# A second output pair whose loads start as places come free, its sums in another place, and output operands at one distance

## The chip, the cores and the metric

The kernel runs on one core of a Trainium2 chip. The metric is the device time of one execution in microseconds. Three runs of the kernel before took 709.29, 709.85 and 711.43 us; the median is 709.85.

## The reference

Linear attention over 4 batches, 8 heads and 576 positions with head dimension 64 (`kv = k^T v`, `out = q kv`, normalised by its root mean square), then two feed-forward layers on the 2304 tokens of width 512. The first has a softmax-weighted hidden layer of 1024 with a layer norm; the second, which the change touches, is this:

```python
a = x @ w_a            # 2304 x 512 times 512 x 1536
b = x @ w_b
return (a * b @ w_out).astype(np.float32)   # 2304 x 1536 times 1536 x 512
```

All of it is float32. Every product is made of three matmuls on numbers split into a high and a low part (`h` times `h`, `h` times `l`, `l` times `h`).

## The kernel before, in words

Three stages follow one another on one core. The first works through 18 token tiles (attention, first layer); its transposed results go to DRAM in `x2d`. The second (`quad`, L719 on) makes `a * b` for three blocks of 768 tokens, `s` = 0, 1, 2, and six slices `j` of the hidden width. The third (`out_pair`, L889 on) multiplies by `w_out`.

In the second and third stage a 2 by 2 block product is made of seven products in place of eight, with sums of the operands' quarters: `XB11, XT1, XT2, XB21, XB22, XT3, XT4` on one side (`XB` are quarters, `XT` sums made of them: XT1 = XT3's quarter - XB11, XT2 = XB22 - XT1, XT4 = XB21 - XT2, and the last, `XT3`, the difference of two quarters), `WA11, WS1, WS2, WA12, WS4, WS3, WA22` on the other.

`quad(j, s, m)` is one of these block products: seven products of 6 matmuls with 384 columns (L715), of which the last, WA22 times XT4, is put off into the next `quad` (`close_quad`, after its third product). `m` = 0 gives `a`, `m` = 1 gives `b`; `times` then multiplies them (VectorE for the first quarter, GpSimd for the others, L756) and stores them in DRAM, `gd[s]` (L758, SP's queue). The tiles of `a` and `b` lie in two pools at the right end of SBUF.

`out_pair(k)` is the same for two token tiles: seven products of 18 matmuls with 256 columns (L886), nine pairs, `pairs` = (s, m) for s in 1, 2, 0. The operands of pair `k` are `g2[k, n]`, a high and a low tile each. Their quarters are loaded from `gd` into the low tile (`g_load`, L831), sums are made on VectorE (`g_steps`, the tiles `e`), the high part is a cast on ScalarE and the low part a subtraction on VectorE (`g_split`, L838 and L557). The pairs use two sets of places in turn: pair 0 has `ga` and places of the weights of stage two, pair 1 the places of `x0`, which is free after `quad(5, 0, 1)`, the last of stage two. `e` of pair 1 lies where `a` and `b` lay.

The order of the work is written out by hand. Each `quad` has six ticks and each `out_pair` six; `then(t4=[...])` hangs steps on a tick of the next `quad`, `ticks` does so for an `out_pair`. Each engine takes its instructions in that order, DMA issues (SP's, ScalarE's) included. The weights `w_out` come as seven sums from DRAM: three into `w1`, which lies in the pool `wo` where the tiles of `x1` lay, and four into `w2`, which lies in the place of `x2`; `half` splits one half of such a weight. The high part of WA22 has a place of its own (`last_hi`, `wo3`).

Of the kernel before, what the change touches and what calls it, by code (L numbers as in the profile page):

```python
# [8 lines left out]
F32 = mybir.dt.float32  # L9
F32R = mybir.dt.float32r  # L10
# [7 lines left out]
DRAM = bass.MemoryType.DRAM  # L18

P = 128  # L20

# [76 lines left out]
def tile_attention_moe(ctx, tc, q, k, v, g_norm, w_in, w_out, g_ln, w_a, w_b, w_out2, out):  # L100
    nc = tc.nc
# [4 lines left out]
    NP = H // 2  # L106
    NK = DM // P
    NF1 = DF1 // P
    NF2 = DF2 // P
    NTILE = NT // P  # L110
    NS = S // P
    FULL = NS * P
    REST = S - FULL
# [5 lines left out]
    TB = SB * P  # L119
    TH = TB // 2  # L120
    NSB = NTILE // SB
    NJ = NF2 // 2
# [18 lines left out]
    gd = [dram.tile([P, 4, SB // 2, NJ, P], F32, name=f"gd{s}") for s in range(NSB)]  # L141
# [4 lines left out]
    def pool(name, bufs, stack=left, side="left", **kw):  # L146
        if side == "right":
            kw["side"] = "right"
        if stack is psum:
            kw["space"] = PSUM  # L150
        return stack.enter_context(tc.tile_pool(name=name, bufs=bufs, **kw))

    def pool_r(name, bufs, stack=None):
        return pool(name, bufs, right if stack is None else stack, "right")
# [7 lines left out]

    wt = pool("wt", 1, top)
    tx = pool("tx", 2, top)
    pool_r("rpad", 1).tile([P, 248], F32, name="rpad")

    xl0 = pool_r("xl0", 1)

# [59 lines left out]
    wo = {}  # L228
# [321 lines left out]
    WA11, WA12, WS3, WA22, WS1, WS2, WS4 = range(7)  # L550
    XB11, XT1, XT2, XB21, XB22, XT3, XT4 = range(7)
    p2 = {}
# [3 lines left out]
    def subtract(eng, out, a, b):  # L556
        eng.tensor_tensor(out=out, in0=a, in1=b, op=ALU.subtract)  # L557
# [164 lines left out]
    def close_quad():  # L722
        if open_quad:
            open_quad.pop()()
# [75 lines left out]
    HD = DM // 2  # L800
    wo2 = {}
    g2 = {}
# [24 lines left out]
        wo2[n] = [t if t is None else t.rearrange("p (j d) -> p j d", j=NJ) for t in (hi, lo)]  # L827
        eng.dma_start(out=wo2[n][1].bitcast(F32), in_=w2d[:, n])

    def g_load(k, n, c=slice(0, NJ), t=None):  # L830

        s, m = pairs[k]
        t = g2[k, n][1].bitcast(F32) if t is None else t
        nc.sync.dma_start(out=t[:, c], in_=gd[s][:, (XB11, XT3, XB21, XB22).index(n), m, c])

    def g_split(k, n, src, c=slice(0, NJ)):
        return [
            lambda: nc.scalar.copy(g2[k, n][0][:, c], src()[:, c]),  # L838
            lambda: subtract(nc.vector, g2[k, n][1][:, c], src()[:, c], g2[k, n][0][:, c].bitcast(F32)),
        ]  # L840
# [4 lines left out]
    def g_steps(k):  # L845

        e = []

        def begin_():
            e.extend(p2["e"].tile([P, NJ, P], F32, tag=f"e{n}", name=f"e{n}") for n in range(2))  # L850
            d(0, XT3, XB11)()

        def d(out, a, b):
            at_ = lambda x: e[-1 - x] if x < 0 else g2[k, x][1].bitcast(F32)
            return lambda: subtract(nc.vector, e[out], at_(a), at_(b))

        def sp(n, at_=None):
            return g_split(k, n, g_raw(k, n) if at_ is None else lambda: e[at_])

        return [  # L860
            begin_, *sp(XB11), d(1, XB22, -1), *sp(XT1, 0), d(0, XB21, -2), *sp(XT2, 1), d(1, XB22, XT3),
            *sp(XB21), *sp(XB22), *sp(XT3, 1), *sp(XT4, 0),
        ]
# [160 lines left out]
    def all_of(steps):  # L1024
        for f in steps:
            f()
# [26 lines left out]
    side = [f for n in ORDER for f in x_split(0, n, lambda n=n: xf[n])]  # L1053
# [35 lines left out]
    left.close()  # L1089
    p2["x2"] = pool("x2", 1, rest)  # L1090

    t = p2["x2"].tile([P, 14 * TB + 32], F32R, tag="x", name="x2")
    t = t[:, :14 * TB].rearrange("p (h n c t) -> p h n c t", h=2, n=7, c=2)
    xs2[2] = [[t[:, h, n] for n in range(7)] for h in range(2)]

# [2 lines left out]
    now, later = by_need[:6], by_need[6:]  # L1098
    for n, (count, which) in enumerate(((1, now), (6, later), (5, now), (2, later))):
        where = pool(f"x1_{n}", 1)  # L1100
        for _ in range(count):
            part, n = which.pop(0)
            x1[part, n] = where.tile([P, 2, TH], F32R, tag=f"x{part}{n}", name=f"x{part}1_{n}")
    xs2[1] = [[x1[part, n] for n in range(7)] for part in "hl"]
    side = [f for n in ORDER for f in x_split(1, n, lambda n=n: xf[n])]
# [6 lines left out]
    side = x_steps(2)  # L1112
# [8 lines left out]
    for j in range(1, NJ - 1):  # L1121
        n = 2 * j + 2
# [16 lines left out]
    te = xl0.tile([P, 3, NJ, P], F32, tag="x3", name="te")  # L1139
    w1, w2 = [], []  # L1140

    def parts(to, t, count):
        size = NJ * HD
        to.extend(t[:, 16 + n * size:16 + (n + 1) * size] for n in range(count))

    def first_place():
        left.close()
        p2["wo"] = pool("wo", 1)
        parts(w1, p2["wo"].tile([P, 16 + 6 * NJ * HD], F32R, tag="w", name="wo1"), 6)
        g2[0, XT2] = place(p2["wo"], "g")  # L1150

    def second_place():
        parts(w2, p2["x2"].tile([P, 14 * TB + 32], F32R, tag="x", name="wo2"), 7)

    def place(where, tag):
        t = where.tile([P, 2, NJ, P], F32R, tag=tag, name="gw")
        return t[:, 0], t[:, 1]

    def g_next(k, n):
# [10 lines left out]
    def half(n, part, eng=nc.vector):  # L1170
        return hi_lo(wo2, n, eng, part)
# [18 lines left out]
    for n, k in ((XB11, 0), (XT1, 1)):  # L1190
# [5 lines left out]
        t1=[gl_(XB11, most), gl_(XT3, most)], t4=[gl_(XB22, most), gl_(XB21, most)], t6=early[:3],  # L1196
# [5 lines left out]
        t1=early[10:12], t3=[first_place], t4=[wl(WA11, w1, 0, nc.scalar), gl_(XB11, last), gl_(XT3, last), gl_(XB22, last), wl(WS1, w1, 1)], t5=[gl_(XB21, last)],  # L1202
# [3 lines left out]
        t2=half(WA11, 0), t3=[wl(WS2, w1, 2), *late_[:4]], t4=half(WA11, 1), t5=late_[4:8], t6=late_[8:],  # L1206
# [3 lines left out]
        t1=half(WS1, 0), t2=half(WS1, 1), t3=[second_place], t4=[wl(WA12, w2, 0, nc.scalar), *half(WS2, 0)],  # L1210
        t5=[wl(WS4, w2, 1, nc.scalar), *half(WS2, 1)], t6=[wl(WS3, w2, 2, nc.scalar), *g_split(0, XT2, lambda: te[:, 1])],
# [3 lines left out]
    def last_operands():  # L1215
        g2[0, XT3], g2[0, XT4] = (place(p2["w", part, 1], "w") for part in "hl")

    def next_loads():
        for n in range(7):
            g2[1, n] = [x0.tile([P, NJ, P], F32R, tag=f"x{part}{n}", name=f"g{part}") for part in "hl"]  # L1220
        for n in (XB11, XT3, XB22, XB21):
            g_load(1, n)

    then(
        t3=[*half(WA12, 0, nc.gpsimd), *half(WA12, 1, nc.gpsimd)],
        t4=[last_operands, *g_split(0, XT3, lambda: te[:, 2])],
        t6=[next_loads, *half(WS4, 0)],
    )
    quad(j, 0, 1)

    def last_places():
        close_quad()
        all_of([*half(WS4, 1), *half(WS3, 0)])
        wo_load(WA22, None, w2[6])
        ab.close()
        p2["o"] = pool_r("o", 5)
        p2["e"] = pool_r("e", 1)
# [10 lines left out]
    side = []  # L1248
    for k in range(len(pairs)):
        counts = [2, 2, 3, 4, 4, 3]  # L1250
        if k == 0:
            side += [*half(WS3, 1), *g_split(0, XT4, lambda: te[:, 0])]
            counts = [0, 4, 4, 4, 4, 2]
        if k + 1 < len(pairs):
            side += g_steps(k + 1)
        ticks = [[side.pop(0) for _ in range(min(n, len(side)))] for n in counts]
        if k == 0:
            ticks[3] += [last_hi, *half(WA22, 0, nc.gpsimd), *half(WA22, 1, nc.gpsimd)]
            out_pair(k, ticks, first_o, last_places)
        else:  # L1260
            out_pair(k, ticks)
# [34 lines left out]
```

## Time and profile before

| what | us |
|---|---|
| median of 3 runs | 709.85 |
| the profiled execution | 709.85 |
| its span, first to last instruction | 708.0 |
| TensorE busy | 677.0 (96%) |
| VectorE busy | 521.8 (74%) |
| GpSimd busy | 305.9 (43%) |
| ScalarE busy | 294.3 (42%) |
| TensorE output products (L886) on the chain that ended last | 17% |

Stage two begins at 285.57 us of the span, the first output product at 566.93, and the last matmul ends at 704.74. The share of busy time counts a matmul from its start to its modelled end, so matmuls overlap in it; how fast they follow each other is read from a window's length and the number of matmuls in it. A wait shows as idle time in front of an instruction, with what released it.

### The profile page before, as it was taken

What the parts mean: (1) busy time and instruction counts of PE and PEld (TensorE: products, weight loads), DVE (VectorE), ACT (ScalarE), POOL (GpSimd) and SP (SyncE); (2) the same over time, 40 slices, a digit from 0 to 9 for tenths busy, and PEclk for the clock granted to TensorE, in tenths of its full rate; (3) what the DMA queues carried; (4) which work ended last, traced back from release to release, by engine and by line L of the source; (5) the groups of instructions that cost most, each with busy time, mean ns of one, the idle gap of its engine ahead of it and who ended that gap; (6) DMA issues with size and microseconds to landing.
All of it is one profiled execution on the core that took longest, in us unless ns stands there. A gap on an engine that the chain in (4) does not pass through costs nothing.

```text
span 708.0 us, 12282 instructions
## 1 busy us (share of the span) xinstructions
PE 677.0 (96%) x4550; PEld 647.8 (91%) x4550; DVE 521.8 (74%) x928; ACT 294.3 (42%) x507; POOL 305.9 (43%) x448
## 2 busy tenths in 40 slices
PE   2599999999999999999999999999999998999998
PEld 2488899999999898899999999999999998999998
DVE  3889977676688776778666866677647979878882
ACT  3668955544455346542321122211222535433431
POOL 2578775677666311114554465554652412000000
PEclk9889999999999999999999999999999999999999
DMA  9997745545542412352434346444345674544521
GB/s 247 315 249 210 191 130 166 153 120 162 165 128 75 135 45 68 105 155 67 143 106 145 116 119 195 141 144 148 116 136 156 241 267 120 158 119 136 148 73 56
DMA packets 107131, 103.83 MB, mean 147 GB/s; under 512 B 25280, under 2 KB 94400, under 8 KB 107072
## 3 DMA queue, kind: packets, MB, share of 16 engines
q1 hardware_dynamic: 101312, 95.18, 45.9%
q10 hardware_dynamic: 5760, 7.87, 3.3%
q8 instruction: 36, 0.59, 0.3%
q14 instruction: 23, 0.19, 0.1%
HBM read 71.05 MB, written 31.98 MB: 146 GB/s over the span
## 4 chain that ended last, share of the span: by engine, by line
PE 76%; DVE 10%; issue 4%; POOL 4%; ACT 3%; DMA 2%; SPq 0%; ACTq 0%; DVEq 0%; POOLq 0%
PE pw L715 28%; PE pq L886 17%; PE x2p L532 5%; PE x2p L530 5%; PE x2p L531 5%; PE ph L445 4%; PE ph L443 4%; PE ph L444 4%; PE ltp L500 2%; PE po L381 1%; PE kvp L349 1%; POOL a L756 1%; DVE nu L92 1%; DMA ring<-in_moe_w_in_dram 1%; PE xtp L418 1%
## 5 line engine op out<-in xcount | busy, mean ns | idle before, releaser
L756 POOL TENSOR_TENSOR a<-b,a 128x384 f32<-128x384 f32 x53 | 63.1, 1205 | 125.0 <-DVE b L745 124.1
L715 PE MATMUL pw<-xh,wh 128*128 128x384 f32 x336 | 114.3, 340 | 1.1 <-DVE b L766 0.3
L715 PE MATMUL pw<-xh,wl 128*128 128x384 f32 x336 | 112.9, 336 | 0.0
L715 PE MATMUL pw<-xl,wh 128*128 128x384 f32 x336 | 112.9, 336 | 0.0
L715 PE MATMUL pw<-x,wh 128*128 128x384 f32 x336 | 85.6, 335 | 0.1
L530 PE MATMUL x2p<-lh,woh 128*128 128x256 f32 x288 | 82.4, 286 | 0.3 <-ACT lh L510 0.2
L531 PE MATMUL x2p<-ll,woh 128*128 128x256 f32 x288 | 80.4, 279 | 0.8 <-DVE ll L513 0.8
L532 PE MATMUL x2p<-lh,wol 128*128 128x256 f32 x288 | 80.4, 279 | 0.5 <-DVE wol L49 0.5
L715 PEld LDWEIGHTS pw<-xh,wh 128*128 128x128 f32 x336 | 63.1, 188 | 4.9 <-DVE b L745 1.6
L715 PEld LDWEIGHTS pw<-xl,wh 128*128 128x128 f32 x336 | 63.1, 188 | 0.0
L715 PEld LDWEIGHTS pw<-xh,wl 128*128 128x128 f32 x336 | 63.1, 188 | 0.0
L715 PEld LDWEIGHTS pw<-x,wh 128*128 128x128 f32 x336 | 60.6, 188 | 0.7 <-DVE b L745 0.4
L886 PE MATMUL pq<-wo,gh 128*128 128x256 f32 x336 | 59.9, 280 | 0.0
L445 PE MATMUL ph<-wih,xl 128*128 128x512 f32 x144 | 57.5, 399 | 1.8 <-DVE xl L428 1.8
L443 PE MATMUL ph<-wih,xh 128*128 128x512 f32 x144 | 58.2, 404 | 0.1
L444 PE MATMUL ph<-wil,xh 128*128 128x512 f32 x144 | 57.4, 399 | 0.0
L715 PE MATMUL pw<-x,wl 128*128 128x384 f32 x168 | 56.2, 334 | 0.0
L531 PEld LDWEIGHTS x2p<-ll,woh 128*128 128x128 f32 x288 | 54.2, 188 | 1.2 <-DVE ll L513 1.2
L530 PEld LDWEIGHTS x2p<-lh,woh 128*128 128x128 f32 x288 | 54.4, 189 | 0.9 <-ACT lh L510 0.5
L886 PE MATMUL pq<-wo,gw 128*128 128x256 f32 x450 | 55.1, 280 | 0.0
L532 PEld LDWEIGHTS x2p<-lh,wol 128*128 128x128 f32 x288 | 54.3, 188 | 0.9 <-DVE wol L49 0.9
L886 PEld LDWEIGHTS pq<-wo,gw 128*128 128x128 f32 x450 | 54.0, 188 | 0.0
(155 smaller groups left out, 1563.8 us busy)
## 6 DMA issues: line engine op xcount, KB each, us to landing
gd<-a SPq DMA_DIRECT2D x72, 192.0 KB, 2.0
ring<-in_moe_w_out_dram SPq DMA_DIRECT2D x20, 512.0 KB, 5.4
gl<-gd SPq DMA_DIRECT2D x16, 384.0 KB, 3.6
gw<-gd SPq DMA_DIRECT2D x12, 384.0 KB, 3.2
ring<-in_moe_w_in_dram SPq DMA_DIRECT2D x8, 512.0 KB, 7.1
qs<-in_q_dram SPq DMA_DIRECT2D x16, 256.0 KB, 6.4
x2d<-x2s ACTq DMA_DIRECT2D x32, 128.0 KB, 1.8
st<-in_moe_w_a_dram SPq DMA_DIRECT2D x8, 512.0 KB, 4.9
```

What stands on the lines that cost most here:

```text
L92: self.nc.vector.scalar_tensor_tensor(out=self.u, in0=self.low, scalar=29, in1=self.u, op0=ALU.logical_shift_right, op1=ALU.bitwise_or)
L349: nc.tensor.matmul(pk, kc[:, j], vt[:, h0:h0 + 2, j, :], start=(j == 0), stop=(j == KJ - 1))
L443: nc.tensor.matmul(ph[:, n, :], xh[:, c, :], wh, start=(c == 0), stop=False)
L444: nc.tensor.matmul(ph[:, n, :], xh[:, c, :], wl, start=False, stop=False)
L445: nc.tensor.matmul(ph[:, n, :], xl[:, c, :], wh, start=False, stop=(c == NK - 1))
L500: nc.tensor.transpose(pt[:, m, :], hs_[i]["so"][:, f * P:(f + 1) * P], ident)
L530: nc.tensor.matmul(pa, wh[:, cs], lh[:, f, :], start=(f == 0), stop=False)
L531: nc.tensor.matmul(pa, wh[:, cs], ll[:, f, :], start=False, stop=False)
L532: nc.tensor.matmul(pa, wl[:, cs], lh[:, f, :], start=False, stop=(f == NF1 - 1))
L715: nc.tensor.matmul(out, wt_[:, wn, c], xt_[xn][:, c], start=first and c == n == 0, stop=c == 1 and n == 2, skip_group_check=not first,)
L756: eng.tensor_tensor(out=a[n], in0=by, in1=a[n], op=ALU.mult)
L886: nc.tensor.matmul(ps, xt_[:, c], wt_[:, c], start=first and c == n == 0, stop=c == NJ - 1 and n == 2, skip_group_check=not first,)
```

## The change

Four things are changed.

- The second pair's loads (`g_load(1, ...)`) no longer stand together on the sixth tick of the last `quad` (`next_loads`). Each place is taken on the tick after the product that read it last (`next_load`): XB11 on tick 1, XB21 on tick 4 (both on SP's queue), XB22 on tick 5 and XT3 on tick 6 (both on ScalarE's queue).
- The sums of the second pair go into `te[:, 2]` and `te[:, 1]` in place of `e0` and `e1`. The tile `te` holds the first pair's sums and is free by then.
- The low parts of WA22 (two halves of 128 x 768) are made by VectorE in the second pair's first tick, no longer by GpSimd from the first pair's fourth tick; ScalarE's casts for them move along.
- Offsets: a pad in front of `x1`, more room behind `x2`, other offsets of `wo`, `gw` and `w2`. A matmul reads a stationary operand (loaded into the array) and a moving one. The distance, here and below, is the moving operand's start address in a partition less the stationary one's, modulo 512 bytes, as the built program has them:

| matmuls | columns | count | before | after |
|---|---|---|---|---|
| first layer in (L443 to L445) | 512 | 432 | 0 | 0 |
| first layer out, `x2p` (L530 to L532) | 256 | 864 | 192 | 192 |
| `quad`, `x0` and `x2` (L715) | 384 | 1008 | 0 | 0 |
| `quad`, `x1` (L715) | 384 | 504 | 128 | 320 |
| output (L886), WA11, WS1 and all but one WS2; WA22 high | 256 | 576 | 192 | 192 |
| output, WA12, WS4, WS3; WA22 low | 256 | 540 | 64 | 192 |
| output, WS2 of the first pair | 256 | 18 | 0 | 192 |

The diff:

```diff
--- before.py
+++ after.py
@@ -18,6 +18,7 @@
 DRAM = bass.MemoryType.DRAM
 
 P = 128
+LINE = 16
 
 
 
@@ -162,7 +163,7 @@
 
     wt = pool("wt", 1, top)
     tx = pool("tx", 2, top)
-    pool_r("rpad", 1).tile([P, 248], F32, name="rpad")
+    pool_r("rpad", 1).tile([P, 120], F32, name="rpad")
 
     xl0 = pool_r("xl0", 1)
 
@@ -827,11 +828,11 @@
         wo2[n] = [t if t is None else t.rearrange("p (j d) -> p j d", j=NJ) for t in (hi, lo)]
         eng.dma_start(out=wo2[n][1].bitcast(F32), in_=w2d[:, n])
 
-    def g_load(k, n, c=slice(0, NJ), t=None):
+    def g_load(k, n, c=slice(0, NJ), t=None, eng=nc.sync):
 
         s, m = pairs[k]
         t = g2[k, n][1].bitcast(F32) if t is None else t
-        nc.sync.dma_start(out=t[:, c], in_=gd[s][:, (XB11, XT3, XB21, XB22).index(n), m, c])
+        eng.dma_start(out=t[:, c], in_=gd[s][:, (XB11, XT3, XB21, XB22).index(n), m, c])
 
     def g_split(k, n, src, c=slice(0, NJ)):
         return [
@@ -847,7 +848,7 @@
         e = []
 
         def begin_():
-            e.extend(p2["e"].tile([P, NJ, P], F32, tag=f"e{n}", name=f"e{n}") for n in range(2))
+            e.extend(p2["e"].tile([P, NJ, P], F32, tag=f"e{n}", name=f"e{n}") if k > 1 else te[:, 2 - n] for n in range(2))
             d(0, XT3, XB11)()
 
         def d(out, a, b):
@@ -1089,7 +1090,7 @@
     left.close()
     p2["x2"] = pool("x2", 1, rest)
 
-    t = p2["x2"].tile([P, 14 * TB + 32], F32R, tag="x", name="x2")
+    t = p2["x2"].tile([P, 14 * TB + 3 * LINE], F32R, tag="x", name="x2")
     t = t[:, :14 * TB].rearrange("p (h n c t) -> p h n c t", h=2, n=7, c=2)
     xs2[2] = [[t[:, h, n] for n in range(7)] for h in range(2)]
 
@@ -1098,6 +1099,8 @@
     now, later = by_need[:6], by_need[6:]
     for n, (count, which) in enumerate(((1, now), (6, later), (5, now), (2, later))):
         where = pool(f"x1_{n}", 1)
+        if n == 0:
+            where.tile([P, 2 * LINE], F32, tag="pad", name="pad")
         for _ in range(count):
             part, n = which.pop(0)
             x1[part, n] = where.tile([P, 2, TH], F32R, tag=f"x{part}{n}", name=f"x{part}1_{n}")
@@ -1141,19 +1144,20 @@
 
     def parts(to, t, count):
         size = NJ * HD
-        to.extend(t[:, 16 + n * size:16 + (n + 1) * size] for n in range(count))
+        to.extend(t[:, n * size:(n + 1) * size] for n in range(count))
 
     def first_place():
         left.close()
         p2["wo"] = pool("wo", 1)
-        parts(w1, p2["wo"].tile([P, 16 + 6 * NJ * HD], F32R, tag="w", name="wo1"), 6)
-        g2[0, XT2] = place(p2["wo"], "g")
+        parts(w1, p2["wo"].tile([P, 6 * NJ * HD], F32R, tag="w", name="wo1"), 6)
+        g2[0, XT2] = place(p2["wo"], "g", 5)
 
     def second_place():
-        parts(w2, p2["x2"].tile([P, 14 * TB + 32], F32R, tag="x", name="wo2"), 7)
-
-    def place(where, tag):
-        t = where.tile([P, 2, NJ, P], F32R, tag=tag, name="gw")
+        parts(w2, p2["x2"].tile([P, 14 * TB + 3 * LINE], F32R, tag="x", name="wo2")[:, 3 * LINE:], 7)
+
+    def place(where, tag, lines=0):
+        t = where.tile([P, lines * LINE + 2 * NJ * P], F32R, tag=tag, name="gw")[:, lines * LINE:]
+        t = t.rearrange("p (h c t) -> p h c t", h=2, c=NJ)
         return t[:, 0], t[:, 1]
 
     def g_next(k, n):
@@ -1215,21 +1219,26 @@
     def last_operands():
         g2[0, XT3], g2[0, XT4] = (place(p2["w", part, 1], "w") for part in "hl")
 
-    def next_loads():
-        for n in range(7):
+    def next_load(n, eng=nc.sync):
+        def load():
             g2[1, n] = [x0.tile([P, NJ, P], F32R, tag=f"x{part}{n}", name=f"g{part}") for part in "hl"]
-        for n in (XB11, XT3, XB22, XB21):
-            g_load(1, n)
+            if n in (XB11, XT3, XB22, XB21):
+                g_load(1, n, eng=eng)
+
+        return load
 
     then(
-        t3=[*half(WA12, 0, nc.gpsimd), *half(WA12, 1, nc.gpsimd)],
-        t4=[last_operands, *g_split(0, XT3, lambda: te[:, 2])],
-        t6=[next_loads, *half(WS4, 0)],
+        t1=[next_load(XB11)], t2=[next_load(XT1)],
+        t3=[next_load(XT2), *half(WA12, 0, nc.gpsimd), *half(WA12, 1, nc.gpsimd)],
+        t4=[next_load(XB21), last_operands, *g_split(0, XT3, lambda: te[:, 2])],
+        t5=[next_load(XB22, nc.scalar)],
+        t6=[next_load(XT3, nc.scalar), *half(WS4, 0)],
     )
     quad(j, 0, 1)
 
     def last_places():
         close_quad()
+        next_load(XT4)()
         all_of([*half(WS4, 1), *half(WS3, 0)])
         wo_load(WA22, None, w2[6])
         ab.close()
@@ -1251,11 +1260,13 @@
         if k == 0:
             side += [*half(WS3, 1), *g_split(0, XT4, lambda: te[:, 0])]
             counts = [0, 4, 4, 4, 4, 2]
+        elif k == 1:
+            side[:0] = [last_hi, *half(WA22, 0), *half(WA22, 1)]
+            counts = [5, 4, 4, 4, 4, 2]
         if k + 1 < len(pairs):
             side += g_steps(k + 1)
         ticks = [[side.pop(0) for _ in range(min(n, len(side)))] for n in counts]
         if k == 0:
-            ticks[3] += [last_hi, *half(WA22, 0, nc.gpsimd), *half(WA22, 1, nc.gpsimd)]
             out_pair(k, ticks, first_o, last_places)
         else:
             out_pair(k, ticks)
```

On SP's queue, at the end of stage two, this stands before. `gd0<-a` are the stores of the last block product (block 0), `gl` and `ga` the loads of quarters of block 1; the four `gl` are the second pair's.

```order
L758 DMA gd2_69<-a21_6082 128x3x128
L758 DMA gd0_67<-a11_6232 128x3x128
L758 DMA gd0_67<-a12_6233 128x3x128
L758 DMA gd0_67<-a22_6235 128x3x128
L834 DMA gl_6373<-gd1_68 128x768
L834 DMA gl_6383<-gd1_68 128x768
L834 DMA gl_6381<-gd1_68 128x768
L834 DMA gl_6379<-gd1_68 128x768
L834 DMA ga_5944<-gd1_68 128x768
L758 DMA gd0_67<-a21_6234 128x3x128
L828 DMA wo2_6273<-w2d_62 128x1536
```

And this now, on the same queue in the same place (lines have moved by one):

```order
L759 DMA gd2_69<-a21_6083 128x3x128
L835 DMA gl_6317<-gd1_68 128x768
L759 DMA gd0_67<-a11_6233 128x3x128
L835 DMA gl_6359<-gd1_68 128x768
L759 DMA gd0_67<-a12_6234 128x3x128
L759 DMA gd0_67<-a22_6236 128x3x128
L835 DMA ga_5945<-gd1_68 128x768
L759 DMA gd0_67<-a21_6235 128x3x128
L829 DMA wo2_6274<-w2d_62 128x1536
```

Two of the four loads stand in front of stores that were in front of them; the other two have gone to ScalarE's queue, between a cast of the first pair and three casts of `wo2`.

On VectorE, in the first pair's second half and the second pair's beginning, this stands before. `e` are the sums, `gl<-..,gh` low parts, `o` additions of finished products.

```order
L557 TENSOR_TENSOR e0_6481<-gl_6383,gl_6373 128x768
L557 TENSOR_TENSOR gl_6373<-gl_6373,gh_6372 128x768
L557 TENSOR_TENSOR e1_6482<-gl_6381,e0_6481 128x768
L557 TENSOR_TENSOR gl_6375<-e0_6481,gh_6374 128x768
L557 TENSOR_TENSOR e0_6481<-gl_6379,e1_6482 128x768
L908 TENSOR_TENSOR o_first_6453<-pq_6412,o_first_6453 128x256
L557 TENSOR_TENSOR gl_6377<-e1_6482,gh_6376 128x768
L557 TENSOR_TENSOR e1_6482<-gl_6381,gl_6383 128x768
L557 TENSOR_TENSOR gl_6379<-gl_6379,gh_6378 128x768
L908 TENSOR_TENSOR o_first_6453<-pq_6460,o_first_6453 128x256
L557 TENSOR_TENSOR gl_6381<-gl_6381,gh_6380 128x768
L557 TENSOR_TENSOR gl_6383<-e1_6482,gh_6382 128x768
```

And this now, from the fifth sum or low part on:

```order
L558 TENSOR_TENSOR te_5946<-gl_6359,te_5946 128x768
L909 TENSOR_TENSOR o_first_6454<-pq_6411,o_first_6454 128x256
L558 TENSOR_TENSOR gl_6345<-te_5946,gh_6344 128x768
L558 TENSOR_TENSOR te_5946<-gl_6375,gl_6387 128x768
L558 TENSOR_TENSOR gl_6359<-gl_6359,gh_6358 128x768
L909 TENSOR_TENSOR o_first_6454<-pq_6461,o_first_6454 128x256
L558 TENSOR_TENSOR gl_6375<-gl_6375,gh_6374 128x768
L558 TENSOR_TENSOR wo2_6274<-wo2_6274,wo3_6580 128x768 x2
L909 TENSOR_TENSOR o1_6578<-pq_6585,o0_6577 128x256
L558 TENSOR_TENSOR gl_6387<-te_5946,gh_6386 128x768
```

The sums stand in `te`; the two low parts of WA22 stand behind the one of XB22, and what followed it comes two instructions later.

## Rows read from the trace of the kernel before

**Rows 1.** The page: busy us (share of the span) xinstructions of each engine.

```profile
PE 677.0 (96%) x4550; PEld 647.8 (91%) x4550; DVE 521.8 (74%) x928; ACT 294.3 (42%) x507; POOL 305.9 (43%) x448
```

**Rows 2.** Chain that ended last, from 571: start us, us, what.

```profile
573.50 3.78 DMA gd<-a
...
577.61 1.79 issue
...
584.60 2.21 DVE gl L557
...
586.83 2.47 DVE e L557
...
590.23 114.51 PE pq L886 x970
```

**Rows 3.** Timeline of PE: start us, us, what, xcount [idle before <-releaser].

```profile
566.93 4.24 PE L886 MATMUL pq<-wo,ga 128*128 128x256 f32 x36
...
572.05 8.67 PE L886 MATMUL pq<-wo,gw 128*128 128x256 f32 x72
...
581.58 0.39 PE L886 MATMUL pq<-wo,gl 128*128 128x256 f32 x1 [0.62 <-DVE gl L557]
...
590.23 0.38 PE L886 MATMUL pq<-wo,gl 128*128 128x256 f32 x1 [0.99 <-DVE gl L557]
...
592.21 2.28 PE L886 MATMUL pq<-wo,gw 128*128 128x256 f32 x18
```

**Rows 4.** Windows of PE: stretch, us, PE busy (x), granted clock, DMA share, GB/s.

```profile
277.10:285.57 8.47, 8.47 (x74) 1.00 0.24 76
297.64:305.81 8.17, 8.17 (x75) 1.00 0.14 48
378.26:402.18 23.92, 23.92 (x140) 1.00 0.54 169
407.43:417.99 10.56, 10.56 (x61) 1.00 0.45 135
566.93:571.00 4.07, 4.07 (x37) 1.00 0.22 65
572.05:574.20 2.15, 2.15 (x19) 1.00 0.90 234
574.20:580.57 6.37, 6.37 (x57) 1.00 1.03 392
592.21:704.58 112.37, 112.37 (x956) 1.00 0.42 124
598.58:602.81 4.23, 4.23 (x38) 1.00 0.70 233
```

**Rows 5.** Timeline of SP: DMA issues.

```profile
551.28 19.55 SPq L758 DMA_DIRECT2D gd<-a  x7
570.92 1.89 SPq L834 DMA_DIRECT2D gl<-gd  x4
```

**Rows 6.** DMA issues: what, engine, xcount, KB each, median us to landing.

```profile
gd<-a SPq DMA_DIRECT2D x72, 192.0 KB, 2.0
...
gl<-gd SPq DMA_DIRECT2D x16, 384.0 KB, 3.6
```

**Rows 7.** Timeline of DVE.

```profile
572.32 0.56 DVE L745 TENSOR_TENSOR b<-pw,b 128x384 f32<-128x384 f32 x1 [2.75 <-PE pw L715]
...
573.39 1.82 DVE L557 TENSOR_TENSOR wo<-wo 128x768 fp32r<-128x768 f32 x2
...
579.50 0.96 DVE L557 TENSOR_TENSOR e<-gl 128x768 f32<-128x768 f32 x1 [1.89 <-issue]
```

**Rows 8.** Timeline of ACT.

```profile
564.58 1.56 ACT L874 CAST wo<-wo 128x768 fp32r<-128x768 f32 x2
...
572.13 0.37 ACT L927 COPY o_first<-pq 128x256 f32<-128x256 f32 x1 [4.95 <-PE pw L715]
```

**Rows 9.** Timeline of POOL.

```profile
584.08 4.41 POOL L557 TENSOR_TENSOR wo<-wo,wo 128x768 fp32r<-128x768 f32 x2 [13.63 <-ACT wo L874]
```

## The prediction, made before the changed kernel ran

> **What bounds the kernel now.** I read the page first, for the engine that is busy: TensorE 96% of the span, the next, VectorE, 74% [rows 1]. A gain must therefore come from TensorE standing less or from its matmuls following each other faster. Then the chain that ended last, in order of time, for the end of the program, the only part whose instructions the change moves [rows 2]: from 573.50 to 590.23 it does not run through TensorE but through a store of `a` (3.78 us), 1.79 us of "issue", and the subtractions of VectorE that make the second output pair's operands; from 590.23 on it is output matmuls alone. Then TensorE's timeline there [rows 3]: three idle times of 0.62 to 0.99 us (the first and the last are shown), each ended by a low part (`gl`) from VectorE. Last the windows, for the pace of matmuls that run without a gap [rows 4]; the granted clock is 1.00 (2.4 GHz) in all nine, so it explains no difference among them.
>
> To get a pace I divide a window by the matmuls that the code puts into it (18 to an output product, 6 to one of `quad`, 24 to a group of `x2p`; the row's x counts also one to three that reach over its edges). With the distances of the table above:
> - 384 columns: 23 products at distance 0, 23.92/138 = 173.3 ns; 10 products of `x1` at 128, 10.56/60 = 176.0 ns.
> - 256 columns: one product at 0, 2.15/18 = 119.4 ns; three at 64, 6.37/54 = 118.0 ns; two at 192, 4.07/36 = 113.1 ns.
> - But `x2p`, all at 192, shows two paces: 8.47/72 = 117.6 ns from 277.10 and 8.17/72 = 113.5 ns from 297.64. And the last 53 output products, where 64 and 192 take turns, run at 112.37/954 = 117.8 ns; two of them at 192, from 598.58, at 4.23/36 = 117.5.
>
> I read this so: at 192 a stream can run at 113.3 ns (mean of the two) or at 117.8, and stays in the one it is in until a gap or another distance throws it out; at 64 only 117.8 was seen. Since the pairs before the change have 64 in every second or third product, they never come back.
>
> The Trainium skill ("TensorE: Matmul & The Clock Gate", section "Step-by-step: what each phase is for") says that TensorE has two independent SBUF read ports and that loading the next weights does not steal bandwidth from the running matmul. By that rule an address could not matter and the whole placement would be worth nothing. The trace disagrees: 113.1, 118.0 and 119.4 ns within 14 us for one form of matmul at one clock [rows 4]. What the rule would make of the time is the second rival.
>
> **The change part by part.** The sum is made against the profiled run, 709.85 us (span 708.0), which is also the median of the three.
>
> *Loads and sums of the second pair.* Before, the four loads stand on SP's queue behind seven stores, from 551.28 to 570.83, and are issued at 570.92 in 1.89 us, 0.47 each [rows 5]. They land 3.6 us after issue [rows 6], and the first sum needs the first two of them, so at about 575.6. VectorE is free for the first sum at 577.61 [rows 2] but sits 1.89 us until 579.50 [rows 7]: not for the loads but for the place, since `e` lies where `a` and `b` lay, and the store of the last `a` must land first. It lands late, after 3.78 us where 2.0 is its kind's median [rows 6], because the DMA engines are full there (share 1.03 from 574.20 [rows 4]). In `te` the sum need not wait for that store: it moves to 577.61. The earlier loads are a second safety, not a term: they cost 2 issues each on SP and ACT, as before in all. On ACT the two issues wait for TensorE's products until 566.93 [rows 3]; behind them stand three casts of `wo2` (0.78 each, 1.56 for two) that ran from 564.58. They end at about 567 + 2 x 0.47 + 2.3 = 570.3, and ACT's next copy is not due before 572.13, after 4.95 us of idling [rows 8]; VectorE waits for TensorE until 572.32 [rows 7]. So this delay is hidden; without that cover it would cost up to 2.5 us. On SP the loads pass stores that wait for GpSimd; they push the stores back by 0.5 us each, and nobody waits for those stores any more.
>
> *Two low parts from GpSimd to VectorE.* GpSimd's two take 4.41 us from 584.08 [rows 9], and just there two VectorE subtractions take 2.21 and 2.47 us [rows 2] instead of 0.91 (1.82 for two) [rows 7]; their pitch is 0.87, 1.82 less the overlap. VectorE gains two of 0.87 and loses 2.9 of stretching: -1.1 us on the chain that TensorE waits for.
>
> What is late next? At 113.3 ns a product takes 2.04 us; from 572.05 [rows 3] the second pair's first four are due at 580.2, 582.3, 584.3, 586.3 and the first pair's last at 588.4. VectorE, from 577.61 with 0.87 a subtraction and 0.34 an add, has their operands after 2, 4, 6 and 8 subtractions (an add before the third and fourth): 579.4, 581.1, 583.2, 584.9; the first moved low part, tenth subtraction after two adds, at 587.0. The slack is 0.8 us or more everywhere, small but enough: I count no idle. From 572.05 to 592.21 are 8 products [rows 3]: 20.16 us now, 8 x 18 x 0.1133 = 16.32 then: **-3.84 us** (3.20 of it idle and restart, the rest pace).
>
> *Output operands at one distance.* All 63 products stand at 192. The first two start at 113.1 behind `quad`'s matmuls at distance 0; the third starts behind six such matmuls too, so I take the fast pace for it, and after it nothing breaks the stream. 53 products: 112.37 - 954 x 0.1133 = **-4.28 us**. If they settle at 117.8: 0.
>
> *`x1` from 128 to 320.* No row shows 320. Over its columns' time at 2.4 GHz (160.0 and 106.7 ns) a matmul took 6.4 (113.1) to 16.0 ns (176.0) more [rows 4]; that bounds it to 166.4 and 176.0 ns, -4.8 to 0 us on 84 products, 504 matmuls. A worse distance is not excluded; that is the fourth rival. I take the nearest row of the same form, 173.3: 504 x 2.7 = **-1.36 us**. It is on the path: `quad`'s stretch is TensorE without gaps, as its windows are [rows 4].
>
> `x0`, `x2`, `x2p` and the first stage keep their distances: nothing. The tail behind the last matmul is untouched. Sum: -3.84 - 4.28 - 1.36 = -9.48, **700.4 us**.
>
> **Rivals.**
> 1. *The slow pace.* The waits go, but the stream at 192 settles at 117.8, as `x2p` did from 277.10. For: both are seen at one distance, and it takes one gap or phase. Against: both starts behind `quad` gave the fast one. 20.16 - 144 x 0.1178 = 3.20, and 1.36: 705.3.
> 2. *Distance decides nothing*, as the rule above has it; the pace depends on something else, say on the idle times that happen to stand before. Then the placement does not do what it says, `x1` included: 709.85 - 3.20 = 706.6.
> 3. *A new wait in the place of the old.* VectorE, with two more subtractions in its order and 0.8 us of slack, comes late once, TensorE stands 1.2 us (an old wait with its restart) and starts again slow: 709.85 - 3.20 - 1.36 + 1.2 = 706.5; fast, 701.6. For: ACT's casts stand between VectorE's, and each hand-over can cost. Against: the row of the new wait would have to lose more than the 1.1 us won back from GpSimd.
> 4. *Slower: `x1` at a bad distance.* It decides from (3.84 + 4.28)/504 = 16.1 ns over today's 176.0, 192 ns, twice the largest addition seen; at 200 ns 504 x 24 = 12.1 us, and 713.8. Against: no gapless window is near it.
>
> **How the numbers follow.** Forecast 0.60, rivals 0.17, 0.08, 0.10, 0.05. The likeliest's own range is 697.0 (all of `x1`'s bound) to 702. Up to 705.9 it takes in rival 1 and the fast half of rival 3; left out are rival 2, the other half of 3, and 4: 0.18. So 697.0 to 705.9. About 0.3%, 2.1 us, is what a measurement of this kernel can tell from no change. All cases but the fourth are faster by more than that, less a little for a third that goes badly: faster 0.92, same 0.04, slower 0.04.
>
> **What would show it.** TensorE without idle from 572 to 590, the chain there output matmuls alone; VectorE's first sum at about 577.6 and no subtraction over 1 us between 578 and 592 (else GpSimd was not the cause); output products 2.04 us apart to the end (2.12 means rival 1 or 2); `x1`'s products 1.04 us apart (1.06 now). It is wrong if a row `pq` waits for `gl` or `wo` once more, or if the pace changes without a gap.

## The result and the profile after

The changed kernel took 701.43, 700.43 and 704.68 us; the median given with them, 703.05, counts a fourth execution too, 1126 us at a mean clock of 0.56, which is left out of the ratio. The kernel before took 709.58 beside it (median of 4). Ratio 0.989, 95% interval 0.9846 to 0.9935: faster by about 1.1%. The profiled execution took 701.43 us.

The page: TensorE's share is what it was [rows 1]; it is busy for 7.3 us less, and GpSimd has two instructions fewer, VectorE two more.

```profile
PE 669.7 (96%) x4550; PEld 640.4 (92%) x4550; DVE 517.8 (74%) x930; ACT 293.7 (42%) x507; POOL 301.3 (43%) x446
```

The end of the chain that ended last. Where [rows 2] had a store, "issue" and VectorE between 571 and 590, there is TensorE alone:

```profile
566.50 4.08 PE pq L887 x36
570.58 1.04 PE pw L716 x6
571.62 124.45 PE pq L887 x1098
```

VectorE's timeline, against [rows 2, 7]: the first sum, the two subtractions that had taken 2.21 and 2.47 us, and the two low parts that came from GpSimd.

```profile
576.94 0.95 DVE L558 TENSOR_TENSOR te<-gl 128x768 f32<-128x768 f32 x1
...
581.93 0.95 DVE L558 TENSOR_TENSOR gl<-te,gh 128x768 fp32r<-128x768 f32 x1
582.92 0.96 DVE L558 TENSOR_TENSOR te<-gl 128x768 f32<-128x768 f32 x1
...
585.86 1.82 DVE L558 TENSOR_TENSOR wo<-wo,wo 128x768 fp32r<-128x768 f32 x2
```

Windows: the stretch, its length, the busy time of TensorE, of its weight loads, of VectorE, ScalarE and GpSimd (with counts), the granted clock, the DMA share, GB/s. In this order the rows are the start; nine products of `x1` (54 matmuls); a block of 42 products of `quad`; the third to the tenth output product (144 matmuls); the other 53 (954).

```profile
0.00:47.64 47.64, 27.74 (x155) 24.31 (x156) 32.52 (x61) 25.77 (x48) 25.56 (x52) 0.93 1.04 278
406.14:415.49 9.35, 9.35 (x55) 9.15 (x55) 4.69 (x9) 3.87 (x6) 7.14 (x6) 1.00 0.51 153
388.44:432.69 44.25, 44.11 (x253) 43.59 (x253) 31.58 (x57) 10.15 (x17) 24.79 (x22) 1.00 0.45 141
571.46:587.78 16.32, 16.32 (x145) 16.32 (x145) 15.84 (x22) 10.14 (x15) 0.00 (x0) 1.00 0.65 189
587.78:695.90 108.12, 108.12 (x956) 108.09 (x954) 85.52 (x119) 41.78 (x63) 0.00 (x0) 1.00 0.43 127
```

The same start and the same block in the kernel before:

```profile
0.00:47.64 47.64, 27.54 (x151) 24.06 (x151) 31.90 (x57) 24.73 (x46) 24.78 (x51) 0.89 1.04 280
389.70:433.95 44.25, 44.19 (x253) 43.87 (x253) 31.58 (x57) 10.15 (x17) 24.78 (x22) 1.00 0.46 138
```

From the first instruction to the last matmul the profiles differ by 8.66 us. Place by place, by the starts of the same matmul in both traces: -1.07 up to 47.64 us (the 151st matmul), -0.44 from there to the start of stage two, +0.92 in stage two (285.57 to 566.93 before, 284.06 to 566.34 now), -3.84 from the third to the eleventh output product, -4.23 to the last one. The last two are two terms of the prediction's sum. The first three are taken up in the section on the prediction.

### The profile page after: what moved, and what is told of

Read it like the earlier page. It is cut to its first block, busy times and chain, and to the rows that moved or that the text cites. A ratio compares the mean times of both kernels' runs of the same rounds, so it can differ in the third digit from the quotient of the medians.

```text
span 699.3 us, 12286 instructions
## 1 busy us (share of the span) xinstructions
PE 669.7 (96%) x4550; PEld 640.4 (92%) x4550; DVE 517.8 (74%) x930; ACT 293.7 (42%) x507; POOL 301.3 (43%) x446
## 4 chain that ended last, share of the span: by engine, by line
PE 79%; DVE 9%; ACT 3%; POOL 3%; issue 3%; DMA 2%; SPq 0%; ACTq 0%; DVEq 0%; POOLq 0%
PE pw L716 29%; PE pq L887 18%; PE x2p L533 5%; PE x2p L531 5%; PE x2p L532 5%; PE ph L446 4%; PE ph L444 4%; PE ph L445 4%; PE ltp L501 2%; PE po L382 1%; PE kvp L350 1%; DMA ring<-in_moe_w_in_dram 1%; DMA wo<-w2d 1%; DVE nu L93 1%; PE xtp L419 1%
## 5 line engine op out<-in xcount | busy, mean ns | idle before, releaser
L532 PE MATMUL x2p<-ll,woh 128*128 128x256 f32 x288 | 80.3, 279 | 0.8 <-DVE ll L514 0.8
L887 PE MATMUL pq<-wo,gh 128*128 128x256 f32 x336 | 57.7, 276 | 0.0
L445 PE MATMUL ph<-wil,xh 128*128 128x512 f32 x144 | 56.7, 394 | 0.0
L532 PEld LDWEIGHTS x2p<-ll,woh 128*128 128x128 f32 x288 | 54.3, 188 | 1.2 <-DVE ll L514 1.2
L887 PE MATMUL pq<-wo,gw 128*128 128x256 f32 x450 | 53.1, 276 | 0.0
L887 PEld LDWEIGHTS pq<-wo,gw 128*128 128x128 f32 x450 | 52.0, 188 | 0.0
```

The source lines that it names most:

```text
L445: nc.tensor.matmul(ph[:, n, :], xh[:, c, :], wl, start=False, stop=False)
L532: nc.tensor.matmul(pa, wh[:, cs], ll[:, f, :], start=False, stop=False)
L887: nc.tensor.matmul(ps, xt_[:, c], wt_[:, c], start=first and c == n == 0, stop=c == NJ - 1 and n == 2, skip_group_check=not first,)
```

## The experiments

Each time is a median and stands beside runs of the kernel before on the same chip; a ratio has its 95% interval behind it. A pace is the time from the start of one matmul to the start of the next. The theory: the address distance sets the pace of gapless output matmuls; the stalls came from the place of the sums and from GpSimd. The main rival: the distance decides nothing.

**The changed kernel again**, for its spread.

> The changed kernel once more, for the spread of its executions, beside which one of 704.7 stood among 700.4 and 701.4. Theory 1 (the start scatters): up to the 150th matmul the profiles so far differ by 2.3 us though the instructions there are the same, so executions lie between 700 and 704, and the profile shows 113.3 ns to the end whatever its time. Theory 2 (the stream at 192 falls into the slow pace in some executions, as in both_back's profile after one gap): executions in two groups, 700 to 702 and 704.5 to 707, and a profile of the second group shows 117.8 ns. There is no gap between 572 and 592 to make it fall, so theory 1 is the likelier.

701.54 to 703.64, median 702.25, before 709.81; ratio 0.9896 [0.9875, 0.9916]. From the third output product on all 1098 matmuls run at one pace: 124.32/1098 = 113.2 ns.

```profile
571.58:695.90 124.32, 124.32 (x1098) 124.32 (x1098) 101.36 (x140) 51.94 (x78) 0.00 (x0) 1.00 0.45 135
```

No second group of times among these six. What made the one of 704.68 has no trace.

**The offsets alone.** The kernel before with all parts of the diff that touch the pads, `wo`, `gw` and `w2`, and none that touch loads, sums and low parts.

```diff
-    pool_r("rpad", 1).tile([P, 248], F32, name="rpad")
+    pool_r("rpad", 1).tile([P, 120], F32, name="rpad")
...
-    t = p2["x2"].tile([P, 14 * TB + 32], F32R, tag="x", name="x2")
+    t = p2["x2"].tile([P, 14 * TB + 3 * LINE], F32R, tag="x", name="x2")
...
-        to.extend(t[:, 16 + n * size:16 + (n + 1) * size] for n in range(count))
+        to.extend(t[:, n * size:(n + 1) * size] for n in range(count))
...
```

> The kernel before with the offsets alone: x1 at 320, all output products at distance 192; loads, sums and low parts as before. If distance sets the pace and a stream at 192 takes its pace anew after each gap: the three idle times of 0.6 to 1.0 us at 581 to 591 stay, the products between run at 113.3 or 117.8 ns, and after the last gap either 113.3 to the end (709.7 - 4.3 - 0.4, about 705) or 117.8 to the end (about 709.5). If distance decides nothing: 117.8 from 592 on as in the kernel before, 709.7. In all cases the x1 products run at 173.3 instead of 176.0 ns; if that is on the path, 1.4 less than just said, if TensorE's later wait for VectorE takes it back, nothing.

705.60, before 710.85; ratio 0.9926 [0.9903, 0.995]. The three idle times of TensorE are all there:

```profile
580.67 0.39 PE L887 MATMUL pq<-wo,gl 128*128 128x256 f32 x1 [1.16 <-DVE gl L558]
...
585.94 0.39 PE L887 MATMUL pq<-wo,gl 128*128 128x256 f32 x1 [0.91 <-DVE gl L558]
...
589.33 0.39 PE L887 MATMUL pq<-wo,gl 128*128 128x256 f32 x1 [1.06 <-DVE gl L558]
```

and yet the 53 products behind them run at 108.01/954 = 113.2 ns:

```profile
591.26:699.27 108.01, 108.01 (x956) 108.01 (x954) 84.83 (x119) 41.87 (x63) 0.00 (x0) 1.00 0.44 129
```

So the pace comes with the addresses, without the waits going.

**All but the offsets.** The changed kernel with the offsets of before (the parts above reversed).

> The changed kernel with the offsets of before: x1 at 128, the output products at 192, 64 and 0. If distance sets the pace: no idle time from 572 to 592, but output products of 2.12 us (117.8 ns) from the fourth on, 709.7 - 3.2 = 706.5. If it is the gaps and not the distance that made the slow pace: 113.3 ns to the end, 709.7 - 3.84 - 4.28 = 701.6.

706.88, before 710.85; ratio 0.9941 [0.992, 0.9963]. No idle time, and on average the slow pace: 111.99/954 = 117.4 ns.

```profile
571.50:588.26 16.76, 16.76 (x145) 16.76 (x145) 16.28 (x23) 10.13 (x15) 0.00 (x0) 1.00 0.66 192
588.26:700.25 111.99, 111.99 (x955) 111.99 (x954) 86.25 (x118) 41.80 (x63) 0.00 (x0) 1.00 0.41 121
```

20.16 - 16.76 = 3.40 us for the waits without the pace (3.20 forecast). The rival is out: the fast pace came with the offsets and the waits still there, and did not come with the waits gone and the offsets not.

Not every product is slow here. Three at 64, three at 192, three at 192 seven products later, and the next three at 192, again seven later, all without a gap:

```profile
573.65:580.01 6.36, 6.36 (x56) 6.36 (x55) 6.26 (x10) 1.83 (x4) 0.00 (x0) 1.00 0.87 244
580.01:586.14 6.13, 6.13 (x56) 6.13 (x55) 6.06 (x9) 5.96 (x9) 0.00 (x0) 1.00 0.35 111
594.62:600.75 6.13, 6.13 (x57) 6.13 (x55) 6.10 (x10) 3.33 (x5) 0.00 (x0) 1.00 0.67 197
609.22:615.58 6.36, 6.36 (x57) 6.36 (x55) 5.53 (x8) 2.58 (x4) 0.00 (x0) 1.00 0.66 203
```

That is 6.13/54 = 113.5 ns twice and 6.36/54 = 117.8 ns the third time: behind products at 64 a stream at 192 can come back to the fast pace, and does not always.

**All output products at 64.**

```diff
+        p2["wo"].tile([P, 24 * LINE], F32, tag="lead", name="lead")
...
-        g2[0, XT2] = place(p2["wo"], "g", 5)
+        g2[0, XT2] = place(p2["wo"], "g", 7)
...
-        parts(w2, p2["x2"].tile([P, 14 * TB + 3 * LINE], F32R, tag="x", name="wo2")[:, 3 * LINE:], 7)
+        parts(w2, p2["x2"].tile([P, 14 * TB + 3 * LINE], F32R, tag="x", name="wo2")[:, 1 * LINE:], 7)
```

> The changed kernel with all output products at distance 64 instead of 192 (x1 at 256 and 384 besides, which by x1_128 does not reach the end). If 64 itself is slow: 117.8 ns from the third product to the end, 16.32 + 108.1 us become 17.0 + 112.4: about 4.9 us slower than the changed kernel, 706.5. If only the taking of turns between 64 and 192 made the slow pace and any one distance is good: 113.3 ns, time of the changed kernel. x1's products at 256 and 384: 173.3 ns if, as 0, 192, 320 and 448, all but 128 have one pace; 384 at 176 if the period is 256 bytes.

707.18, before 710.39; ratio 0.9956 [0.9939, 0.9973]; 129.20/1098 = 117.7 ns. One distance for all is not enough; 64 is slow by itself.

```profile
575.30:704.50 129.20, 129.20 (x1098) 129.20 (x1098) 102.50 (x140) 51.82 (x78) 0.00 (x0) 1.00 0.44 129
```

**At 160 and at 224**, in the same way.

> The changed kernel with all output products at distance 160 instead of 192. If the pace is a matter of the 64-byte line that the two addresses stand in (64 and 192 are one line and three), 160, half a line off, gives one of the paces seen, 113.3 or 117.8 ns: time of the changed kernel or 4.9 us more. If it goes by the distance itself, it lies between 128 (bad at 384 columns, 176 ns) and 192: 113.3 to 119.4 ns, 0 to 6.5 us more. A pace under 113.3 would make it faster than both, by 1.1 us per ns.

> The changed kernel with all output products at distance 224 instead of 192. By the line: 113.3 or 117.8 ns as at 160. By the distance itself, if the period is 256 bytes, it lies between 192 (113.3) and 256, that is 0 (119.4): 113.3 to 119.4 ns, 0 to 6.5 us more than the changed kernel. A pace under 113.3 would make it faster than both, by 1.1 us per ns.

708.26 [0.9948, 0.9981] and 708.29 [0.9952, 0.9985], before 711.12; 118.6 and 118.2 ns. Neither is better, and 32 bytes to either side of 192 the gain in pace is gone. The 64-byte line in which an address lies does not decide either: by it, one of the two known paces (113.3 or 117.8) was expected at both.

```profile
571.43:701.60 130.17, 130.17 (x1098) 130.17 (x1098) 102.61 (x140) 51.80 (x78) 0.00 (x0) 1.00 0.44 129
```

```profile
573.03:702.84 129.81, 129.81 (x1099) 129.81 (x1098) 102.61 (x140) 51.83 (x78) 0.00 (x0) 1.00 0.43 129
```

**`x1` back at 128.**

```diff
-            where.tile([P, 2 * LINE], F32, tag="pad", name="pad")
+            where.tile([P, 7 * LINE], F32, tag="pad", name="pad")
```

> The changed kernel with x1 back at distance 128 (a pad of 448 bytes in front instead of 128), nothing else. The x1 products run at 175.7 to 176.8 ns again instead of 173.3. If the term of the prediction is on the path: 1.36 us slower than the changed kernel. If it is taken back where TensorE waits for VectorE's sum b once per block of 42 products, those waits get shorter by what the products lose: within 0.3 us of the changed kernel. Output products at 113.3 ns to the end if that pace is stable; 117.8 in some executions would explain the one run of 704.7 of the changed kernel.

702.41, ratio 0.9886 [0.9859, 0.9913]: no difference from the changed kernel that the times show, though 1.36 us would fit into the intervals. The traces decide. Nine products of `x1` are at 9.51/54 = 176.1 ns again, and the block of 42 products takes what it takes at 320 and what it took before:

```profile
405.77:415.28 9.51, 9.51 (x56) 9.51 (x56) 4.89 (x9) 3.88 (x6) 7.12 (x6) 1.00 0.48 150
388.04:432.30 44.26, 44.20 (x254) 43.88 (x253) 31.56 (x57) 10.15 (x17) 24.78 (x22) 1.00 0.45 137
```

What sets the block is a stretch in which VectorE works without a break, shown here in the changed kernel. Its first instruction is released by ScalarE (which waits for GpSimd), 24.03 us behind the block's start (24.02 with `x1` at 128), and TensorE, which waits for the `b` at the stretch's end, goes on at 420.08:

```profile
412.47 1.36 DVE L67 TENSOR_SCALAR st<-st 128x512 f32<-128x512 f32 x1 [2.46 <-ACT st L62]
...
418.89 0.67 DVE L93 SCALAR_TENSOR_TENSOR st<-st 128x512 uint32<-128x512 uint32 x1
419.49 0.54 DVE L746 TENSOR_TENSOR b<-pw,b 128x384 f32<-128x384 f32 x1
```

**`x1` at 192 and 448**, by pads of 256 bytes in front of its second and its third pool and none in front of the first.

```diff
-        if n == 0:
-            where.tile([P, 2 * LINE], F32, tag="pad", name="pad")
+        if (0, 4, 4, 0)[n]:
+            where.tile([P, (0, 4, 4, 0)[n] * LINE], F32, tag="pad", name="pad")
```

> The changed kernel with x1 at two other distances: XB11, XT1, XT2 and XT4 at 192, XB21, XB22 and XT3 at 448. If distance acts by its place within 512 bytes, the two have different paces; if within 256, one pace. If 192 is good for 384 columns as it is for 256 (6.6 ns over the columns' time), 166.6 ns a matmul, else 173 to 176. The time is that of the changed kernel within 0.5 us if x1's pace is hidden by the waits for VectorE; 288 x 6.7 = 1.9 us less or more if 192 alone is at 166.6 and on the path, 3.4 us if both are.

702.95, ratio 0.9883 [0.9858, 0.9907]. The median is 173.3 ns at 192 and 173.8 at 448, over all products, those that contain waits too; so 192 is no better than 0 for 384 columns. In the run at 64 above, `x1` stood at 256 (173.3) and 384 (176.7).

**Low parts back on GpSimd.**

```diff
-        elif k == 1:
-            side[:0] = [last_hi, *half(WA22, 0), *half(WA22, 1)]
-            counts = [5, 4, 4, 4, 4, 2]
...
+            ticks[3] += [last_hi, *half(WA22, 0, nc.gpsimd), *half(WA22, 1, nc.gpsimd)]
```

> The changed kernel with WA22's two low parts on GpSimd again, from the first pair's fourth tick. Theory: GpSimd's 4.4 us stretch two VectorE subtractions by 2.9 us together and VectorE saves 1.74 us, so its chain comes 1.1 us later than in the changed kernel, where it is 0.75 to 1.1 us ahead of TensorE: subtractions over 2 us at about 584 to 589, TensorE idle 0 to 0.6 us once or twice, and the pace stays at 113.3 ns, since place_only kept it through three gaps: 0 to +0.8 us. Rival (GpSimd was harmless, the stretching came from DMA traffic or from the late place): no subtraction over 1 us, no idle, time as the changed kernel.

704.05, ratio 0.9923 [0.9899, 0.9948]. Two VectorE subtractions and GpSimd's pair run at the same time, and the subtractions are as long as before the change again:

```profile
584.03 2.27 DVE L558 TENSOR_TENSOR gl<-te,gh 128x768 fp32r<-128x768 f32 x1
586.34 2.48 DVE L558 TENSOR_TENSOR te<-gl 128x768 f32<-128x768 f32 x1
```

```profile
583.61 4.39 POOL L558 TENSOR_TENSOR wo<-wo,wo 128x768 fp32r<-128x768 f32 x2 [11.68 <-ACT wo L875]
```

TensorE stands 0.17 and 1.05 us for it, and the eight products take 18.12 us instead of 16.32: 1.80 more, over twice what I had expected at most. The error: the 1.74 us that VectorE saves lie behind the operands that come late, so these bear the whole 2.9 of stretching, less the 1.0 us by which the second pair's fourth operand was ahead in the changed kernel. The second stretched subtraction ends at 588.82, 0.82 us behind GpSimd's last (588.00), about its own length without GpSimd (0.95). The Trainium skill ("SBUF — State Buffer", section "SBUF: two separate sides") says that a VectorE operation with two SBUF inputs and a GpSimd operation that reads SBUF shut each other out for a whole instruction; this trace agrees.

**Sums back in `e0`, `e1`; loads back at the last tick; both.**

```diff
-            e.extend(p2["e"].tile([P, NJ, P], F32, tag=f"e{n}", name=f"e{n}") if k > 1 else te[:, 2 - n] for n in range(2))
+            e.extend(p2["e"].tile([P, NJ, P], F32, tag=f"e{n}", name=f"e{n}") for n in range(2))
```

```diff
-        t5=[next_load(XB22, nc.scalar)],
-        t6=[next_load(XT3, nc.scalar), *half(WS4, 0)],
+        t6=[next_loads, *half(WS4, 0)],
...
```

> The changed kernel with the second pair's sums in e0 and e1 again, which lie where a and b lay. Theory (the place was what the first sum waited for): the first sum starts when the last store of a has landed, about 578.9 on the changed kernel's clock instead of 576.94, 2.0 us later; VectorE was 0.75 to 1.1 us ahead of TensorE, so TensorE is idle for 0.9 to 1.3 us in all, once or twice, between 579 and 588, at 113.3 ns otherwise: +0.9 to +1.3 us. Rival (the early loads alone did it, the place was free in time): no idle, +0.

> The changed kernel with the second pair's four loads together on SP at the last tick again, as before the change; te, the low parts and the offsets stay. Prediction's claim (the early loads are a second safety and not a term): the loads land at 574 to 576, the first sum starts at about 577, TensorE has no idle time: within 0.3 us of the changed kernel. Rival (the loads are what made the sums early): the first sum starts at 578 or later and TensorE stands 0.5 us or more.

> The changed kernel with the four loads together on SP at the last tick and the sums in e0 and e1, both as before the change; low parts of WA22 on VectorE and offsets stay. Theory (either of the two edits is enough, e_back and loads_late each cost nothing): without both the first sum waits for the last store of a again and starts 7.4 us after the third output product instead of 5.5; TensorE, to which VectorE had 0.75 to 1.1 us of lead, is idle for 0.9 to 1.3 us in all; from the third to the eleventh product 17.2 to 17.8 us instead of 16.32, all products between at 113.3 ns: about 1.2 us slower than the changed kernel. Rival (neither edit had a part in it, GpSimd's low parts alone made the stalls): first sum at 5.5 us, no idle, time of the changed kernel.

702.00 [0.9867, 0.9904] and 701.82 [0.9859, 0.9898], before 710.39: each alone costs nothing and leaves TensorE without idle time, where 0.9 to 1.3 us were expected for the sums; the first sum starts 5.48 us behind the third output product in both, as in the changed kernel. With both back: 704.10 [0.9892, 0.9951], before 711.12, and the sum starts 7.69 us behind the third output product:

```profile
581.07 0.96 DVE L558 TENSOR_TENSOR e<-gl 128x768 f32<-128x768 f32 x1 [2.13 <-issue]
```

What ties the two together is the last store of `a`. The issue rows (last number: us from issue to landing), with the sums alone back, with both back, and in the kernel before:

```profile
gd<-a SPq DMA_DIRECT2D x1, 192.0 KB, 2.0
```

```profile
gd<-a SPq DMA_DIRECT2D x1, 192.0 KB, 6.1
```

```profile
gd<-a SPq DMA_DIRECT2D x1, 192.0 KB, 5.8
```

With early loads the DMA engines have room when it is issued (busy 57% of the 0.5 us around its issue, 89% with both back), and the place is free in time. With late loads it lands late (6.7 us with the loads alone back), but sums in `te` do not wait for it. No subtraction of the second pair takes over 1 us in any of the three, which leaves GpSimd's pair, absent in them, as the cause of the stretching.

The profile with both back shows more than was asked for. TensorE stands once:

```profile
583.14 0.39 PE L887 MATMUL pq<-wo,gl 128*128 128x256 f32 x1 [1.21 <-DVE gl L558]
```

and the stream, at 192 like in the changed kernel, leaves that gap in the other pace: 8.16/72 = 113.3 ns ahead of it, 112.25/954 = 117.7 behind, to the end.

```profile
573.38:581.54 8.16, 8.16 (x73) 8.16 (x73) 5.73 (x9) 3.05 (x5) 0.00 (x0) 1.00 1.01 355
...
591.49:703.74 112.25, 112.25 (x956) 112.25 (x954) 87.08 (x120) 41.84 (x63) 0.00 (x0) 1.00 0.42 123
```

This execution took 709.38 us; four of the other five took 703.0 to 704.3, one 707.4. The gap costs 1.55 us in its product, the pace behind it 4.2; the eight products take 18.11 us, where 17.2 to 17.8 were expected.

## Why the prediction was right, and where it was not

**What bounds.** Right. The stalls and the pace of the output products made 8.07 of the 8.66 us.

**The eight products: forecast -3.84, measured -3.84.** 16.32 us as worked out, no idle time, the sum at 576.94 where 577.6 was named. Of the causes, GpSimd's part is right but was taken too small: returned alone it costs 1.80. "VectorE gains two of 0.87 and loses 2.9 of stretching: -1.1" sets a gain that comes later against a loss that comes first. The store as the cause is right, the DMA traffic that made it late too, but its row was misread: 3.78 us is what the chain gives it, up to 577.28, and a landing there would not hold up a sum until 579.50. By the issue row the store landed 5.8 us after 573.50, at 579.3. And to have `te` as the term and the early loads as "a second safety" is only half of it. Either does, and only without both does the gap come back (1.55).

**The pace: forecast -4.28, measured -4.23.** That a stream at 192 is fast or slow, and one at 64 slow, held in every trace: of nine profiles with all products at 192, eight were fast to the end, and one fell after a gap. A gap can throw the stream out, as forecast, but mostly does not: of the six gaps in fast streams (three with the offsets alone, two with the low parts back, one with both edits back) one did. Rival 1 exists; where all output products stand at 192 it took a gap, and the changed kernel has none. What does not hold is "they never come back": with the offsets of before and no gap, products at 192 came back twice. So products at 64 between those at 192 do not by themselves keep a stream slow, and what decides its pace behind them stays open.

**`x1`: forecast -1.36, measured 0.** The size was right: 173.3 for 176.0 ns. The step of the prediction that failed is "It is on the path: `quad`'s stretch is TensorE without gaps, as its windows are". The windows I had chosen [rows 4] were gapless because I looked for such. In the blocks of stage two TensorE waits for VectorE's `b`, and what `x1` wins is given back there: in the block shown 0.20 us over its 12 products without a wait, against 0.08 and 0.09 more in the two products (110 and 113 of stage two, counted from 0) that wait, and the rest where distances change. The block is 44.25 us with either distance, since VectorE's stretch hangs on GpSimd and ScalarE and not on `x1`'s pace.

**The sum.** 700.4 forecast, 702.25 by the median of the six later executions. With `x1` worth nothing the sum is 709.85 - 8.12 = 701.7. That the profiled 701.43 comes nearer to 700.4 than that is luck: the lost 1.36 and stage two's +0.92 were for the most part made up by a start and first stage that were 1.51 us shorter, and the start differs from profile to profile with the same instructions, as the last section shows. Stage two's +0.92 can't be laid to one part of the change. 0.52 of it, in product 239, stands in all 13 profiles other than that of the kernel before (0.50 to 0.54), those with the offsets alone and with all but the offsets among them (0.53 each), which share no edit; with one profile of the kernel before it stays open which is the usual case. 0.42 in product 66 and 0.33 in product 235 differ among the 13 from -0.25 to 0.42 and from 0 to 0.59.

## What to carry to other kernels

Before a faster pace is counted, look once per period of the loop for the wait that ends it. If the engine waited for was released by something other than the faster stretch, the gain only makes that wait longer. Where two edits each free the same resource, undo them together as well as apart, since each alone can look worthless. And where matmuls of one form show two paces at one clock, compare the start addresses of their two operands before looking for a cause in time.

## What was not expected of the hardware

- **Pace by distance** (moving less stationary start address; TensorE at 2.4 GHz). 256 columns: 0 119.4 ns, 64 117.7, 160 118.6, 192 113.3 or 117.8, 224 118.2. 384 columns: 173.3 at 0, 192, 256, 320 and 448 (there 173.8), 176.0 to 176.7 at 128 and 384. So the best distance depends on the columns. In the built programs the stationary operand of all these matmuls starts at a multiple of 512 bytes, but for the one product of 256 columns at distance 0, where both operands start at 192: its 119.4 ns, against 113.3 with the moving operand alone at 192, is the only row that tells the distance from the moving operand's own address. What in the memory or the array does this, no run here tells.
- **The pace is a state.** At 192 one gap of 1.21 us changed it for the remaining 120 us, with no other difference on TensorE. The last 72 matmuls of `x2p`, at 192 in every kernel and behind the same two waits (0.24 and 0.34 us), show it too: 113 ns a step in ten of the 14 profiles and 118 in four. From the first start to the last, 71 steps, in the changed kernel and in the one with the offsets alone:

```profile
296.12:304.16 8.04, 8.04 (x73) 8.04 (x72) 6.02 (x7) 3.63 (x6) 0.00 (x0) 1.00 0.14 49
```

```profile
296.16:304.52 8.36, 8.36 (x73) 8.36 (x72) 6.03 (x7) 3.62 (x6) 0.00 (x0) 1.00 0.13 47
```

- **The start scatters.** The 151st matmul came at 46.4 to 48.8 us in the 14 profiles, with the DMA engines full in all of them (share 1.02 to 1.04). Where the mean granted clock was 0.96 of full speed in the first 48 us it came at 46.5 to 46.8 (five profiles), at 0.93 at 46.4 to 46.7 and once at 48.1, at 0.89 at 47.6 and 47.8, and the latest, 48.84, at 0.86 (`x1` at 192 and 448):

```profile
0.00:47.64 47.64, 26.62 (x143) 23.58 (x144) 30.86 (x54) 23.71 (x44) 23.49 (x50) 0.86 1.03 281
```

Two executions can thus differ by 2.4 us before any instruction that was changed has run. The clock and the start go together; which makes which, no run here tells.
